# First quad's k and q loaded as f32 on two hardware queues, k in natural key order, batch-0 masks added on TensorE

## The chip, the cores and the metric

One core of one Trainium2 chip. The metric is the device time of one execution in microseconds (us). Nearly all executions of one kernel agree within 1%. Each ratio uses runs on the same chip in the same rounds. The jobs ran on different chips, so medians of two jobs compare only roughly, and the ratios to the kernel before are the better guide.

## The reference

Two stages, one after the other: attention of eight batches with eight heads, 512 local and 32 global positions each, then a two-layer MoE block of 512 to 2048 to 512 on the 4352 rows.

```python
k_all = np.concatenate([k_g, k_l], axis=2); v_all = np.concatenate([v_g, v_l], axis=2)
out_g = sm(scale * q_g @ k_all^T) @ v_all                    # global rows see every key
mask  = np.abs(pos[:, None] - pos[None, :]) <= 32            # local rows: a band ...
s_ll  = np.where(mask, scale * q_l @ k_l^T, -1e9)
out_l = sm(concat([scale * q_l @ k_g^T, s_ll])) @ v_all      # ... and all global keys
h = x @ w_in                                                 # x: out_g and out_l by rows
out = (h * sigmoid(1.702 * h)) @ w_out
```

## The kernel before

Four heads are a *quad*; a batch has two, `a` and `c`. Each engine executes its instructions in the order in which they are written, so an instruction that waits holds up all behind it on its engine (below, a cast that waits 4.3 us holds up a transpose whose input had been ready for 1.9). The attention of batch 0 has no MoE work to lie beside, so TensorE is not full until it is done. Its calls: Tk transposes of k, S scores, X exponential, M mask, K/XK global keys, ekU/U sums and outputs.

```python
    # loads of batch 0: q of quad 0 as f32 by hardware, k by software DMA (gpsimd)
    nc.scalar.dma_start(out=q32, in_=qf[0][:, 0])
    load_g32(0, "qk")                       # small q_g, k_g as f32, on SP's hardware queue
    load_g32(0, "v", eng=nc.scalar)         # small v_g as f32, on ACT's hardware queue
    for j in range(4):
        load_k(0, 0, j)
    ...
        def Tk(self, cs=(0, 1, 2, 3)):      # k: 32x32 transposes on VectorE
            ...
            nc.vector.transpose(self.kT[:, cs], rk[:, cs])          # contiguous write
        ...
        def M(self, rnd, lo=0, hi=LW):      # mask: multiplies the exponentials on VectorE
            e = self.E[rnd][:, :, at + lo : at + hi]
            nc.vector.tensor_mul(e, e, mask[...].to_broadcast(...))
    ...
    # start of batch 0 (S scores, X exponential, K/XK global keys, ekU/U sums and outputs)
    a.S(0)
    a.X(0)
    a.S(1, split=True, warm=4)
    a.X(1)
    c.ext()
    cast_g32(0, "v")                        # v_g -> bf16 tile rvg, on VectorE
    c.Tk()
    a.K(); a.XK(); a.M(0)
    c.Tq(); c.gg(); c.S(0); c.X(0)
    a.M(1)
    ...                                     # eg, c.K
    a.ekU(0); ... a.U(0); a.R()
    a.ekU(1, 3)                             # first TensorE reader of rvg
    c.S(1); c.X(1, halves=True)
    ...                                     # rest of a's and c's outputs, then MoE of batch 0
```

The softmax here doesn't subtract the row's maximum and nothing guards it: scores larger than these inputs give would overflow.

Of the kernel before, what the change touches and what calls it, by code (L numbers as in the profile page):

```python
# [20 lines left out]
def kernel(  # L21
# [43 lines left out]
    kf = k_l.rearrange("b (u j) (c r t) d -> b j r u c (t d)", j=4, c=4, t=4)  # L65
    vf = v_l.rearrange("b h (c r t) d -> b t r h c d", c=4, t=4)
# [6 lines left out]
    def load(b, us=(0, 1), kq=True):  # L73
        if b not in loaded:
            loaded[b] = (ld.tile([128, 2, 4, 4 * D], BF16, name="rk"),
                         ld.tile([128, 2, 16 * D], BF16, name="rq"))
        if kq:
            for j in (0, 2, 1, 3):
                for u in us:
                    load_k(b, u, j)  # L80
            load_q(b, us)

    def load_k(b, u, j):
        nc.gpsimd.dma_start(out=loaded[b][0][32 * j : 32 * j + 32, u], in_=kf[b, j][:, u])  # L84

    def load_q(b, us):
        s = slice(us[0], us[-1] + 1)
        nc.gpsimd.dma_start(out=loaded[b][1][:, s], in_=qf[b][:, s])
# [3 lines left out]
    def load_v(b, us=(0, 1)):  # L92
        s = slice(us[0], us[-1] + 1)
        hs = slice(4 * us[0], 4 * us[-1] + 4)
        for t in (0, 2, 1, 3):
            p = slice(32 * t, 32 * t + 32)
            nc.gpsimd.dma_start(out=vtiles[b % 2][p, s, :, :, :D], in_=vf[b, t][:, hs])  # L97
# [17 lines left out]
    def load_g32(b, names, hold=False, eng=None):  # L115
        for name, s in (("q", qgf), ("k", kgf), ("v", vgf)):
            if name in names:
                t = g32[b, name] = consts.tile([128, 2, D], F32, name="g32%s%d" % (name, b))
                if hold:
                    nc.vector.memset(t[:, :, 0:1], 0.0)  # L120
                if name == "v":
                    load_turned(eng or nc.sync, t, s[:, 2 * b : 2 * b + 2, :])
                else:
                    (eng or nc.sync).dma_start(out=t, in_=s[:, 2 * b : 2 * b + 2, :])

    def cast_g32(b, names):
        for name, t in (("q", rqg), ("k", rkg), ("v", rvg)):
            if name in names:
                if b:
                    nc.scalar.activation(t[:, 2 * b : 2 * b + 2, :D], g32[b, name], AF.Copy)  # L130
                else:
                    nc.vector.tensor_copy(t[:, 2 * b : 2 * b + 2, :D], g32[b, name])

    load(0, kq=False)
    q32 = ld.tile([128, 16 * D], F32, name="q32", bufs=1)
    nc.scalar.dma_start(out=q32, in_=qf[0][:, 0])
    load_g32(0, "qk")
    load_g32(0, "v", eng=nc.scalar)
    for j in range(4):
        load_k(0, 0, j)  # L140


    mk = consts.tile([32, 208], BF16)
    nc.vector.memset(mk, 1.0)
    for sg, base in ((1, 2 * W + 3), (-1, -3)):
        nc.gpsimd.affine_select(
            out=mk, in_=mk, pattern=[[-sg, 208]], compare_op=ALU.is_ge,
            fill=0.0, base=base, channel_multiplier=4 * sg,
        )
# [14 lines left out]
    keep(62, psP.tile([128, 512], F32, name="w", tag="p"), 128)  # L164
# [9 lines left out]
    mb = consts.tile([128, 16, 12], BF16)  # L174
# [3 lines left out]
    def make_mb():  # L178
        for k in range(4):
            nc.vector.tensor_copy(mb[32 * k : 32 * k + 32],  # L180
                                  mk[:, 3 - k : 195 - k].rearrange("p (r t) -> p t r", t=16))

    def make_mask():
        at = 0
        for c, (r0, nr) in enumerate(WIN):
            lo = r0 - 8 * c + 2
            nc.scalar.activation(
                mask[:, c // 2, at : at + 16 * nr].rearrange("p (t r) -> p t r", t=16),
                mb[:, :, lo : lo + nr], AF.Copy)
            at = (at + 16 * nr) % LW  # L190

    ones32 = consts.tile([128, 32], BF16)
    nc.vector.memset(ones32, 1.0)
    nc.vector.memset(rvg[:, :, D:], 1.0)
    bd = consts.tile([128, 4, 32], BF16)
    nc.vector.memset(bd, 0.0)
    for j in range(4):
        r = (j + 1) % 4
        nc.vector.memset(bd[32 * r : 32 * r + 32, j, :], 1.0)
    for i in range(2):  # L200
        v = consts.tile([128, 2, 4, 4, D + 2], BF16, name="v%d" % i)
        nc.vector.memset(v[:, :, :, :, D:], 1.0)
        vtiles.append(v)
# [10 lines left out]
    def load_rest():  # L214
        load_v(0)
        for part in range(2):
            cs = slice(part * (d_ff // 2), (part + 1) * (d_ff // 2))
            for u in range(2):
                nc.gpsimd.dma_start(out=w_in_sb[:, part, 2 * u : 2 * u + 2, :], in_=w_in_r[u][:, :, cs])
        for g4 in range(4):  # L220
            nc.gpsimd.dma_start(
                out=w_out_sb[:, 4 * g4 : 4 * g4 + 4, :].rearrange("p (g e) m -> p g (e m)", e=2),
                in_=w_out_r[:, 2 * g4 : 2 * g4 + 2, :])
            if g4 == 1:
                load(1, (0,))
        load(1, (1,))
        load_v(1, (0,))
        load_v(1, (1,))
        load(2)
# [7 lines left out]
    class Quad:  # L237
        def __init__(self, Q):
# [10 lines left out]
            self.E = [None, None]  # L249
            self.st = {}  # L250
# [3 lines left out]
        def Tk(self, cs=(0, 1, 2, 3)):  # L254
            if cs[0] == 0:
                self.kT = att.tile([128, Sl], F32, name="kT", bufs=3)
                self.k = self.kT.bitcast(BF16).rearrange("p (m e) -> p m e", e=2)
            rk = loaded[self.b][0][:, self.u].bitcast(F32).rearrange("p c w -> p (c w)")
            cs = slice(128 * cs[0], 128 * cs[-1] + 128)
            nc.vector.transpose(self.kT[:, cs], rk[:, cs])  # L260
# [16 lines left out]
        def S(self, rnd, split=False, warm=0):  # L277
            if split:
                ps = [pbank("s") for _ in range(4)]
                keep(warm, ps[0])  # L280
            else:
                pt = self.spt(rnd)
                ps = [pt[:, j, :] for j in range(4)]
            off = 0
            for c in (2 * rnd, 2 * rnd + 1):
                r0, nr = WIN[c]
                t0, n = (0, 4, 1, 4)[c], (20, 19, 19, 20)[c]
                for e in range(2):
                    for j in range(4):
                        p = slice(32 * j, 32 * j + 32)  # L290
                        nc.tensor.matmul(  # L291
                            ps[j][:, off : off + n * nr],
                            lhsT=self.k[p, 128 * c : 128 * c + 128, e],
                            rhs=self.q[p, t0 : t0 + n, r0 : r0 + nr, e],
                            start=(e == 0), stop=(e == 1), skip_group_check=True,
                        )
                off += n * nr
            if split:
                self.gk(ps[2][:, RW : RW + 32], self.qg)
            self.ps = ps if split else pt  # L300
            self.E[rnd] = att.tile([128, 4, RW + 32], BF16, name="e%d" % rnd)
# [12 lines left out]
        def X(self, rnd, halves=False):  # L314
# [6 lines left out]
            for lo, hi in ((0, 228), (228, RW)) if halves else ((0, RW),):  # L321
                nc.scalar.activation(e[:, :, lo:hi], self.ps[:, :, lo:hi], AF.Exp, scale=scale)  # L322
# [3 lines left out]
        def M(self, rnd, lo=0, hi=LW):  # L326
            at = 36 if rnd else 40
            e = self.E[rnd][:, :, at + lo : at + hi]
            nc.vector.tensor_mul(e, e, mask[:, rnd : rnd + 1, lo:hi].to_broadcast([128, 4, hi - lo]))  # L329
# [184 lines left out]
    rk, rq = loaded[0]  # L514
    def cast_q(hf):
        f = slice(512 * hf, 512 * hf + 512)
        nc.scalar.activation(rq[:, 0, f], q32[:, f], AF.Copy)

    make_mb()
    cast_q(0)  # L520
    cast_q(1)
    make_mask()
    cast_g32(0, "q")
    transpose_g(0, 2, "q")
    a.ext((0, 1))
    a.Tq(0, 8)
    a.Tq(8, 16)
    a.Tk((0, 1))
    a.ext((2, 3))
    a.Tk((2, 3))  # L530
    cast_g32(0, "k")
    transpose_g(0, 2, "k")
    load_rest()
    a.S(0)
    a.X(0)
    a.S(1, split=True, warm=4)
    a.X(1)
    c.ext()
    cast_g32(0, "v")
    c.Tk()  # L540
    a.K()
    a.XK()
    a.M(0)
    c.Tq()
    c.gg()
    c.S(0)
    c.X(0)
    a.M(1)
    load_g32(1, "qkv", hold=True)
    a.eg()  # L550
    c.K(0)
    a.ekU(0)
    c.K(1)
    c.XK()
    a.U(0)
    a.R()
    a.ekU(1, 3)
    c.S(1)
    c.X(1, halves=True)
    a.ekU(2, 4)  # L560
    a.U(1)
    a.U(2)
    a.Gm()
    c.M(0)
    a.XL(0)
    c.M(1, 0, 192)
    c.M(1, 192)
    a.XL(1)
# [25 lines left out]
    for fc in range(4, FC):  # L594
        h_step(0, fc)
        if fc == 7:
            cast_g32(1, "qkv")
        if fc == 10:
            transpose_g(2, 4)
# [13 lines left out]
    a.T()  # L613
    a.ext()
# [160 lines left out]
```

## Time and profile before

| | before |
|---|---|
| median of 3 runs | 312.8 us (312.46 to 313.14) |
| span of the profiled run | 310.7 us |
| first exponential starts | 8.61 us |
| MoE of batch 0 starts on TensorE | 20.19 us |
| from that moment to the end | 290.5 us |

After 20.19 us TensorE has next to no hole (its list of waits holds 0.3 us of them), so a change in the start shows in the moment at which MoE starts, and what is left (span less that moment) should stay at 290.5. In some traces the record of MoE's first matmul is missing, so that 15 matmuls stand beside 16 weight loads; the start is then that of the first weight load. Where both are recorded they start together.

### The profile page before, as it was taken

What the parts mean: (1) busy time and instruction counts of PE and PEld (TensorE: products, weight loads), DVE (VectorE), ACT (ScalarE), POOL (GpSimd) and SP (SyncE); (2) the same over time, 40 slices, a digit from 0 to 9 for tenths busy, and PEclk for the clock granted to TensorE, in tenths of its full rate; (3) what the DMA queues carried; (4) which work ended last, traced back from release to release, by engine and by line L of the source; (5) the groups of instructions that cost most, each with busy time, mean ns of one, the idle gap of its engine ahead of it and who ended that gap; (6) DMA issues with size and microseconds to landing.
All of it is one profiled execution on the core that took longest, in us unless ns stands there. A gap on an engine that the chain in (4) does not pass through costs nothing.

```text
span 310.7 us, 7885 instructions
## 1 busy us (share of the span) xinstructions
PE 302.8 (97%) x3257; PEld 148.6 (48%) x3257; DVE 210.4 (68%) x463; ACT 167.3 (54%) x254; POOL 80.0 (26%) x131
## 2 busy tenths in 40 slices
PE   7899999999999999999999999999999999999995
PEld 6444444444554454444454455444454454446653
DVE  7887946869867866776957866776767855574320
ACT  4817465476536744565446735565556652563321
POOL 8822579677146000900045001200000000000000
PEclk9999999999999999999999999999999999999999
DMA  8999999999969212970279113901120012201123
GB/s 154 149 189 207 206 161 193 165 147 129 151 77 168 45 36 61 139 108 12 60 77 169 30 36 71 102 0 31 41 49 23 0 38 55 48 0 29 41 61 76
DMA packets 60099, 27.44 MB, mean 88 GB/s; under 512 B 43296, under 2 KB 51744, under 8 KB 60064
## 3 DMA queue, kind: packets, MB, share of 16 engines
q0 software_dynamic: 51536, 17.11, 50.7%
q1 hardware_dynamic: 7904, 9.12, 11.9%
q10 hardware_dynamic: 624, 0.72, 0.8%
q8 instruction: 25, 0.41, 0.5%
q14 instruction: 10, 0.08, 0.1%
HBM read 35.13 MB, written 8.91 MB: 142 GB/s over the span
## 4 chain that ended last, share of the span: by engine, by line
PE 91%; DVE 3%; ACT 2%; DMA 1%; POOL 1%; issue 0%; ACTq 0%; DVEq 0%; POOLq 0%
PE op L482 37%; PE hp L457 36%; PE s L291 6%; PE ov L389 5%; PE ov L367 3%; DMA rk<-in_k_l_dram 1%; PE s L457 1%; ACT e L322 1%; PE kb L310 1%; DVE e L329 1%; PE op L494 1%; PE s L310 1%; DVE gT L465 1%; PE s L406 1%; POOL rk L84 1%; PE ov L162 1%
## 5 line engine op out<-in xcount | busy, mean ns | idle before, releaser
L482 PE MATMUL op<-w_out_sb,gT 128*128 128x512 bf16 x528 | 121.9, 380 | 0.1
L465 DVE SCALAR_TENSOR_TENSOR gT<-th,hp 128x512 bf16<-128x512 f32 (+1 forms) x140 | 91.1, 655 | 43.0 <-ACT th L464 42.4
L457 PE MATMUL hp<-xL,w_in_sb 128*128 128x512 bf16 x496 | 108.6, 379 | 0.3 <-DVE xL L421 0.3
L464 ACT ACTIVATE th<-hp 128x512 f32<-128x512 f32 (+1 forms) x140 | 79.9, 573 | 43.7 <-PE hp L457 41.2
L457 PEld LDWEIGHTS <-w_in_sb 128*128 128x128 bf16 x576 | 56.1, 98 | 65.1 <-issue 1.2
L482 PEld LDWEIGHTS <-gT 128*128 128x128 bf16 x528 | 49.3, 98 | 56.2 <-issue 3.3
L322 ACT ACTIVATE e<-s 128x1712 bf16<-128x1712 f32 (+2 forms) x32 | 49.6, 1552 | 15.8 <-PE s L406 8.9
L496 ACT ACTIVATE ob<-op 128x512 f32<-128x512 f32 (+2 forms) x35 | 20.5, 585 | 61.6 <-PE op L482 59.1
L97 POOL DMA_DIRECT2D v<-in_v_l_dram x36 | 27.0, 757 | 96.2 <-PE s L406 88.9
L84 POOL DMA_DIRECT2D rk<-in_k_l_dram x64 | 34.9, 557 | 12.3 <-DMA w_in_sb<-in_moe_w_in_dram 4.7
L329 DVE TENSOR_TENSOR e<-e,mask 128x1408 bf16<-128x1408 bf16 (+2 forms) x33 | 28.0, 851 | 6.9 <-ACT e L322 6.7
L412 DVE STREAM_TRANSPOSE sT<-ov 128x512 f32<-128x512 f32 x16 | 11.4, 714 | 31.3 <-PE ov L389 31.3
L291 PE MATMUL s<-q,kT 32*128 32x200 bf16 (+1 forms) x512 | 21.3, 284 | 1.5 <-DVE kT L260 0.9
L421 DVE TENSOR_TENSOR xL<-ov,rs 128x512 bf16<-128x512 f32 x32 | 20.7, 685 | 2.2 <-PE ov L389 0.9
L291 PEld LDWEIGHTS <-kT 32*128 32x128 bf16 x512 | 10.9, 95 | 14.7 <-issue 9.1
L357 ACT ACTIVATE ek<-kb 128x512 bf16<-128x512 f32 x16 | 9.6, 600 | 8.4 <-PE kb L310 8.4
L389 PE MATMUL ov<-e,v 128*32 128x192 bf16 (+1 forms) x512 | 13.1, 240 | 0.0
L416 DVE STREAM_TRANSPOSE rs<-rT 128x512 f32<-128x512 f32 x16 | 11.4, 711 | 0.6
L260 DVE STREAM_TRANSPOSE kT<-rk 128x512 f32<-128x512 f32 (+1 forms) x17 | 11.4, 671 | 0.0
L263 DVE STREAM_TRANSPOSE q<-rq 128x512 f32<-128x512 f32 (+1 forms) x17 | 10.9, 647 | 0.0
L389 PEld LDWEIGHTS <-v 128*32 128x32 bf16 x512 | 9.8, 97 | 2.0 <-issue 2.0
L310 PE MATMUL kb<-q,kgT 32*32 32x512 bf16 x128 | 10.0, 385 | 0.5 <-ACT e L319 0.5
(71 smaller groups left out, 155.5 us busy)
## 6 DMA issues: line engine op xcount, KB each, us to landing
out_dram<-ob SPq DMA_DIRECT2D x132, 64.0 KB, 1.7
rk<-in_k_l_dram POOLq DMA_DIRECT2D x64, 64.0 KB, 4.0
v<-in_v_l_dram POOLq DMA_DIRECT2D x28, 128.0 KB, 4.5
rq<-in_q_l_dram POOLq DMA_DIRECT2D x6, 512.0 KB, 6.7
w_in_sb<-in_moe_w_in_dram POOLq DMA_DIRECT2D x4, 512.0 KB, 11.7
w_out_sb<-in_moe_w_out_dram POOLq DMA_DIRECT2D x4, 512.0 KB, 13.4
rq<-in_q_l_dram POOLq DMA_DIRECT2D x3, 256.0 KB, 7.9
q<-in_q_l_dram ACTq DMA_DIRECT2D x1, 512.0 KB, 3.9
```

Of the source, the lines that this page charges most:

```text
L84: nc.gpsimd.dma_start(out=loaded[b][0][32 * j : 32 * j + 32, u], in_=kf[b, j][:, u])
L97: nc.gpsimd.dma_start(out=vtiles[b % 2][p, s, :, :, :D], in_=vf[b, t][:, hs])
L291: nc.tensor.matmul(ps[j][:, off : off + n * nr], lhsT=self.k[p, 128 * c : 128 * c + 128, e], rhs=self.q[p, t0 : t0 + n, r0 : r0 + nr, e], ...
L322: nc.scalar.activation(e[:, :, lo:hi], self.ps[:, :, lo:hi], AF.Exp, scale=scale)
L329: nc.vector.tensor_mul(e, e, mask[:, rnd : rnd + 1, lo:hi].to_broadcast([128, 4, hi - lo]))
L389: nc.tensor.matmul(ov[32 * j : 32 * j + 32, :].rearrange("p (t r) -> p t r", t=16)[:, :, r0 : r0 + nr], lhsT=lv, rhs=self.E[c // 2][:, j, ...
L421: nc.vector.tensor_mul(self.x[:, 2 * self.u + h, :], self.st[1 + h], self.st["rs"])
L457: nc.tensor.matmul(hp[:, : width(i)], lhsT=w_in_c[:, fc // 8, kc, fc % 8 // 2, :, fc % 2], rhs=(xL[i] if i < B else xG)[:, kc, :], start=( ...
L464: nc.scalar.activation(th[:, :n], hp[:, :n], AF.Tanh, scale=0.851)
L465: nc.vector.scalar_tensor_tensor(gTs[i][:, fc, :n], in0=th[:, :n], scalar=1.0, in1=hp[:, :n], op0=ALU.add, op1=ALU.mult)
L482: nc.tensor.matmul(op, lhsT=gTs[i][:, fc, tci * 128 : tci * 128 + 128], rhs=w_out_sb[:, fc, :], start=(first and fc == 4 * f4), stop=(fc = ...
L496: nc.scalar.activation(ob[:, lo:hi], op[:, lo:hi], AF.Copy, scale=0.5)
```

## The change

Its intent: start earlier. k of the first quad no longer comes by software DMA; k and q come as f32 in halves on both hardware queues. k lies in natural key order, so its transposes write with a step of 16 elements. The masks of batch 0 are added before the exponential, as a bias matmul on TensorE, in place of a multiplication on VectorE after it. The core of the diff:

```diff
-    kf = k_l.rearrange("b (u j) (c r t) d -> b j r u c (t d)", j=4, c=4, t=4)
+    kf = k_l.rearrange("b (u j) (r t) d -> b (j r) u (t d)", j=4, t=16)
 ...
-    nc.scalar.dma_start(out=q32, in_=qf[0][:, 0])
-    load_g32(0, "qk")
-    load_g32(0, "v", eng=nc.scalar)
-    for j in range(4):
-        load_k(0, 0, j)
+    load_g32("q", qgf)
+    for eng, f in ((nc.scalar, halves[0]), (nc.sync, halves[1])):
+        eng.dma_start(out=k32[:, f], in_=kf[0][:, 0, f])
+        eng.dma_start(out=q32[:, f], in_=qf[0][:, 0, f])
+    load_g32("k", kgf)
 ...
-            nc.vector.transpose(self.kT[:, cs], rk[:, cs])
+            nc.vector.transpose(self.kT.rearrange("p (r t) -> p t r", t=16)[:, lo:hi], rk...)
 ...
+        def B(self, rnd, split=False):      # bias: identity x band, opens the accumulation
+                    nc.tensor.matmul(ps[j][...], lhsT=ident, rhs=near(bias, c), start=..., stop=False)
 ...
     a.ext((2, 3))
-    a.Tk((2, 3))
-    cast_g32(0, "k")
+    load_g32("v", vgf, hold=True)           # hold: a memset on VectorE must run first
+    cast_g32("k", rkg)
     transpose_g(0, 2, "k")
     load_rest()
-    a.S(0)
+    a.B(0)
+    a.B(1, split=True)
+    a.S(0, added=True, part=0)
+    a.S(0, added=True, part=1)
     a.X(0)
-    a.S(1, split=True, warm=4)
+    a.S(1, split=True, added=True)
     a.X(1)
+    c.Tk()
     c.ext()
-    cast_g32(0, "v")
-    c.Tk()
+    c.Tq()
+    cast_g32("v", rvg)
+    c.B(0)
     a.K()
     a.XK()
-    a.M(0)
 ...  (quad c's second round likewise; mask copies moved into MoE of batch 0; the second
      batch's small rows by software DMA; v and w_in in other pieces)
```

## The prediction

> **What bounds the kernel now.** I read the page first: the busy table and its 40 slices.
>
> ```profile
> PE 302.8 (97%) x3257; PEld 148.6 (48%) x3257; DVE 210.4 (68%) x463; ACT 167.3 (54%) x254; POOL 80.0 (26%) x131
> PE   7899999999999999999999999999999999999995
> DMA  8999999999969212970279113901120012201123
> ```
>
> TensorE is the bound, and from the second slice on it has no hole; the DMA engines are full in the first 11 slices (85 us). The change cannot touch the MoE matmuls, which are most of the 302.8 us, so it can only bring forward the moment at which TensorE becomes continuously busy with useful work. The page counts the warming matmuls of L162 as busy, so I looked for that moment in the chain in order of time:
>
> ```profile
> 1.35 1.73 POOL rk L84 x3
> 3.08 3.98 DMA rk<-in_k_l_dram
> 7.13 0.38 DVE q L263
> 7.51 0.34 DVE kT L260
> 7.90 0.69 PE s L291 x16
> 8.61 1.61 ACT e L322
> 10.24 0.89 DVE e L329
> ...
> 17.59 0.88 DVE e L329 x2
> 18.51 0.25 PE ov L389 x4
> ...
> 20.26 3.56 PE s L457 x16
> ```
>
> The first scores wait for k (software DMA, landing at 7.06), then two short transposes; the first useful matmul is at 7.90. From there to 20.2, where MoE of batch 0 starts, the chain goes back and forth between the engines; two of its links are mask multiplications (L329). After 20.2 nearly every link is PE: what the change gains must be gained before 20.2. The timeline of the same stretch gives ScalarE and the second quad:
>
> ```profile
> 8.61 1.60 ACT L322 ACTIVATE e<-s 128x1712 bf16<-128x1712 f32 x1 [1.65 <-PE s L291]
> 10.15 1.81 ACT L319 ACTIVATE e<-s 128x428 bf16<-128x428 f32 x4
> 11.83 0.63 ACT L357 ACTIVATE ek<-kb 128x512 bf16<-128x512 f32 x1
> 12.52 1.60 ACT L322 ACTIVATE e<-s 128x1712 bf16<-128x1712 f32 x1
> 15.19 1.66 ACT L322 ACTIVATE e<-s 128x912 bf16<-128x912 f32 x2 [0.49 <-PE s L291]
> 17.51 0.95 DVE L329 TENSOR_TENSOR e<-e,mask 128x768 bf16<-128x768 bf16 x2
> 20.19 3.63 PE L457 MATMUL s<-xL,w_in_sb 128*128 128x512 bf16 x16
> ```
>
> ScalarE is packed from 8.61 to 14.7 (first exponential to the second XK), pauses 0.49, and ends the last exponential at 16.85. Then two mask pieces (ending at 18.46) and 1.73 us of TensorE (half of the sums, then units 1 and 2) lead to 20.19.
>
> Last, whether weights are there when TensorE comes for them. The view of the tile w_in_sb in the first 40 us:
>
> ```profile
> DMA to landing us min/median/max: 8.4/11.7/14.9
> ```
>
> The four transfers were issued from 10.39 to 12.49; the last lands at about 12.49 + 14.9 = 27.4. TensorE needs that one (second half of the columns, kc 2) at 24.03 + 16 x 0.217 + 2 x 0.217 = 27.9. So weights arrive half a microsecond ahead.
>
> **What the Trainium skill says.** ScalarE: Activation LUTs, What ACT_TABLE_LOAD costs: an ACTIVATE with immediate scale and bias takes 186 ns + 0.833 ns an element. For 1712 elements that is 1.61 us; the trace has 1.60. VectorE: DVE Perf Modes, The perf-mode tier table: a copy from f32 in SBUF runs at 2 elements a cycle, tensor_tensor on bf16 at 2 and on f32 at 1. The trace agrees for the mask (1408 elements, 0.873 us mean, 0.62 ns each). DMA: Bandwidth & Descriptors, Issuing engines are not separate DMA queues: transfers from all three queues run on the same 16 engines and interleave, so using two hardware queues saves issue time only. The trace before cannot test it; its hardware queue moved at up to 384 GB/s in the microsecond 3 to 4. The same page, Specifications: below 512 B a transfer does read-modify-write; the page here counts 43296 of 60099 packets under 512 B, and in 6 to 9 us (512 B pieces of k) the engines moved only 117 to 127 GB/s.
>
> **Part by part.**
> *First loads.* Before: q (512 KB, f32) by hardware, k by four software DMAs, 6 to 7.06. After: k and q as f32, four pieces of 256 KB, k first. Bytes: 1.05 MB and 0.13 MB of small q_g and k_g. By the slices, 0.56 MB were moved by 4.0 us, and the rate then was 384 GB/s. k (0.59 MB with q_g) is thus there at about 4.3 to 4.7; the rest, 0.6 MB at 384 GB/s, at 5.6, and as the second quad's software DMAs now start at about 3.0 and share, I take 5.5 for q's first half and 5.9 for its second.
> *ScalarE.* Three casts of 128x512 at 0.6 us (before: two): k at 4.35 and 4.96, q's first half 5.55 to 6.15.
> *VectorE.* Transposes of k's halves (0.42 each) end at 6.0. Cast of q's second half: from the 128x128 casts (182 ns) and 2 elements a cycle I estimate 0.38 us, 6.0 to 6.4. Transposes of q 6.4 to 6.8 and 6.8 to 7.15. Scores' last part ends at 7.5, first exponential starts at **7.6 in place of 8.61: gain 1.0**. k's transposes now write with a step of 16 elements. They are 0.70 us for the contiguous form; the before kernel's strided read (L180, 192 elements in 0.324 us) shows little penalty, so I keep 0.70.
> *ScalarE's run* is unchanged: from the first exponential to the second XK's end took 14.69 - 8.61 = 6.08.
> *Masks of batch 0.* VectorE loses 0.89 + 0.89 + 0.85 + 0.95 = 3.6 us of multiplications and 1.3 us of mask building (L180), ScalarE 1.07 us of mask copies; four mask copies come back in MoE of batch 0, where it idles about 0.27 us a step. Only the last 0.95 us plus two waits, 16.85 to 18.46 = 1.61 us, lies on the path.
> *Bias on TensorE.* 32 matmuls with 128x128 weights, about 0.089 us each by the 62 warming ones (5.49 us), so 0.7 us a round, 2.8 in all. Rounds 1 and 2 fall into the wait for q; warming is shortened by 22 matmuls (1.9 us) and loses its later 11. Round 3 lies beside an exponential. Only the last round is on the path: its PSUM banks come free when the second quad's first exponential is done, 5.72 after the first one's start. Bias 0.7, then scores to exponential 0.72 (14.47 to 15.19 before): start at 7.17, where before it was 6.58. The exponential in one piece takes 1.6, ends at 8.77 against 8.24 before.
> *Sum.* MoE starts 8.77 + 0.05 + 1.73 = 10.55 after the first exponential, before 20.19 - 8.61 = 11.58: gain 1.03. With the 1.0 from the loads, MoE starts at **7.6 + 10.55 = 18.15, which is 2.04 us earlier**.
> *Weights.* k by 4 KB in place of 1 KB at the source, the hardware start, and no four-piece loads ahead: q of the second quad lands near 8.2 against 10.6, so the stream behind it runs about 2.4 us earlier, and w_in's last part lands near 25. It is needed at 25.9. The first 512 columns come first and land near 15, long before 18.15.
> *Later batches.* Same arithmetic; k's DMAs go from 64 to about a dozen, off the path. The only TensorE holes after 35 us sum to about 0.5 us (40 to 70 us), and of these I give the change 0.2 us. VectorE now transposes batch 1's global rows just before its scores, 0.44 us, in about 0.5 us of slack.
> Total: 2.04 + 0.2 = 2.2; 312.8 - 2.2 = **310.6 us**.
>
> **The rivals.**
> (a) *The f32 loads land late.* Twice the hardware bytes, and now shared with the second quad's software DMAs. For it: the small g32 loads, sharing with q32, took 4.3 us to land. If q lands at 6.9, the exponential starts at 8.6, and only the mask's 1.03 is left: 311.6.
> (b) *Weights become the wait.* TensorE comes 2 us earlier, but with 0.5 us to spare before, anything that keeps the DMA stream at its old times gives back 1.5 of the 2.0: 312.2. For it: DMA is full for 85 us. Against: the stream starts with fewer, larger pieces.
> (c) *Bias matmuls eat the gain.* If they run at half that rate, or are held by their banks, the last round costs 1.4, not 0.7, and the result is 311.3. Against: the warming matmuls of the same shape of weights do 0.089.
> (d) *Strided transposes are slow.* If writing with a step doubles k's 0.70, the second quad's scores slip by some 0.3 us and the first by up to 0.4; later batches have VectorE at 68%: 311.3.
> (e) *All goes better:* q lands at 5.2, which gives another 0.5, and the 40 to 70 us holes close: 309.8.
>
> **Range and chances.** Most rivals subtract 0.7 to 1.6 from a gain of 2.2 and one adds 0.8; run noise is 0.35. So 309.3 to 312.0 for 8 in 10. Faster by over 2% needs 6.3 us, half of all there is between 7.9 and 20.2: 0.03. Slower by over 2% would need a hole in steady state: 0.02. Within: 0.95.
>
> **What would show it.** Right: k's casts from about 4.4, first exponential at 7.6 (7.3 to 8.1), ScalarE packed from there, bias of the last round about 0.7 us just after the second quad's first exponential, no VectorE mask before 30 us, first L457-type matmul at 18.2 (17.4 to 18.8), and a steady state without new holes. Wrong: q landing after 6.5; a wait on w_in_sb or w_out_sb between 18 and 42 us; k's transposes at 1 us or more; a hole after 50 us.

## The result, and the profile after

| | before | after |
|---|---|---|
| median of runs of the same rounds | 312.97 us (312.46 to 314.58) | 316.74 us (315.88 to 317.53) |
| ratio after / before | | 1.0111, 95% interval 1.0063 to 1.0159 |
| span of the profiled run | 310.7 us | 315.5 us |
| first exponential starts | 8.61 us | 9.19 us |
| MoE starts | 20.19 us | 24.16 us |
| from there to the end | 290.5 us | 291.3 us |

Slower by 1.1%: within 2%, as the prediction held likely, but 6 us from its 310.6 and outside its range. A ratio here and below is the mean time of one kernel's fast runs over that of the other's fast runs of the same rounds, so not quite the ratio of the medians quoted.

The page of the changed kernel, the rows that answer to those of before (busy time by engine, then tenths in 40 slices of 7.9 us):

```profile
PE 303.6 (96%) x3272; PEld 149.3 (47%) x3272; DVE 210.6 (67%) x447; ACT 167.7 (53%) x251; POOL 55.9 (18%) x90
PE   6779999999999999999999999999999999999994
PEclk9779999999999999999999999999999999999999
DMA  7999999999139511990149312900211012200222
```

The steady state looks as before. The second and third slices differ: TensorE is 0.7 busy there, and its granted clock, 0.9 in every slice before, is 0.7. The chain of waits of the changed kernel, in order of time (start, us, what), over the same stretch:

```profile
1.80 5.73 DMA q<-in_q_l_dram
...
9.25 8.03 DMA g32v<-in_v_g_dram
...
24.23 3.56 PE s L460 x16
```

Two transfers carry it in this stretch: q's second half, which the prediction had, and **g32v**, the 64 KB of v_g, which it did not. Its second part is issued at 9.25 and takes 8.03 us. The timeline shows what stood behind it (start, us, engine, line, tiles; in brackets the idle time before and what ended it):

```profile
9.19 1.60 ACT L325 ACTIVATE e<-s 128x1712 bf16<-128x1712 f32 x1 [2.56 <-PE s L295]
10.75 0.23 DVE L117 CAST rkg<-g32k 128x128 bf16<-128x128 f32 x1 [1.92 <-DMA g32k<-in_k_g_dram]
17.39 0.23 DVE L117 CAST rvg<-g32v 128x128 bf16<-128x128 f32 x1 [4.32 <-DMA g32v<-in_v_g_dram]
17.67 0.40 PE L370 MATMUL ov<-ek,rvg 32*32 32x512 bf16 x4 [1.94 <-DVE rvg L117]
20.30 1.60 ACT L325 ACTIVATE e<-s 128x1712 bf16<-128x1712 f32 x1 [3.74 <-PE s L295]
24.16 3.63 PE L460 MATMUL s<-xL,w_in_sb 128*128 128x512 bf16 x16
```

VectorE stood 4.3 us before a cast of 0.23 us; TensorE then stood 1.9 us before the first matmul that reads rvg; and ScalarE, which the prediction had packed, waited 3.7 us for the scores written behind it. The view of all that TensorE waited for (us in total, times, longest):

```profile
PE ov L370 <- DVE rvg L117: 1.9, 1, 1.9
PE s L314 <- DVE kgT L201: 1.7, 1, 1.7
PE s L295 <- DVE q L257: 1.5, 1, 1.5
PE s L295 <- DVE q L267: 0.4, 1, 0.4
```

The second line is the other small load, g32k. The DMA issues of the first 10 us (size, median us to landing) have both:

```profile
g32k<-in_k_g_dram SPq DMA_DIRECT2D x1, 64.0 KB, 8.5
g32v<-in_v_g_dram SPq DMA_DIRECT2D x1, 48.0 KB, 7.9
```

Before, issued at 0.8 to 1.8 us, they took 4.2 to 4.7, and the cast of v_g waited for nothing:

```profile
9.00 0.22 DVE L132 CAST rvg<-g32v 128x128 bf16<-128x128 f32 x1
```

One more line of the profile of before, which the prediction does not use, had the warning: the same load for batch 1, issued on SP's queue at 13 to 15 us, took 13.1 us to land, where nobody waited for it.

Weights were not the wait: no matmul of MoE waited for w_in_sb; its transfers landed 8.8 to 11.9 us after their issue at 6.8 to 13.3:

```profile
DMA to landing us min/median/max: 8.8/9.8/11.9
```

### The profile page after: what moved, and what is told of

It reads as the page before. It is cut to its first block, busy times and chain, and to the rows that moved or that the text cites. A ratio compares the mean times of both kernels' runs of the same rounds, so it can differ in the third digit from the quotient of the medians.

```text
span 315.5 us, 7823 instructions
## 1 busy us (share of the span) xinstructions
PE 303.6 (96%) x3272; PEld 149.3 (47%) x3272; DVE 210.6 (67%) x447; ACT 167.7 (53%) x251; POOL 55.9 (18%) x90
## 4 chain that ended last, share of the span: by engine, by line
PE 88%; DMA 4%; DVE 3%; ACT 1%; SPq 0%; issue 0%; ACTq 0%; DVEq 0%
PE op L485 36%; PE hp L460 34%; PE s L295 6%; PE ov L392 5%; PE ov L370 3%; DMA g32v<-in_v_g_dram 3%; DMA q<-in_q_l_dram 2%; PE s L460 1%; DVE gT L468 1%; PE kb L314 1%; PE op L497 1%; PE s L314 1%; PE s L409 1%; ACT e L325 1%; DVE q L257 0%; ACT th L467 0%
## 5 line engine op out<-in xcount | busy, mean ns | idle before, releaser
L325 ACT ACTIVATE e<-s 128x1712 bf16<-128x1712 f32 x31 | 49.5, 1597 | 20.3 <-PE s L409 8.9
L89 POOL DMA_DIRECT2D v<-in_v_l_dram x32 | 23.8, 754 | 129.1 <-PE s L409 116.0
L332 DVE TENSOR_TENSOR e<-e,mask 128x1408 bf16<-128x1408 bf16 x28 | 24.4, 871 | 5.5 <-ACT e L325 5.5
L295 PE MATMUL s<-q,kT 32*128 32x228 bf16 (+5 forms) x528 | 21.6, 285 | 1.9 <-DVE q L257 1.5
L253 DVE STREAM_TRANSPOSE kT<-rk 128x512 f32<-128x512 f32 (+1 forms) x17 | 16.9, 992 | 1.0 <-ACT rk L518 0.9
L370 PE MATMUL ov<-ek,rvg 32*32 32x512 bf16 x128 | 10.6, 384 | 1.9 <-DVE rvg L117 1.9
L257 DVE STREAM_TRANSPOSE q<-rq 128x512 f32<-128x512 f32 (+1 forms) x17 | 10.8, 640 | 0.0
L314 PE MATMUL kb<-q,kgT 32*32 32x512 bf16 x128 | 10.8, 413 | 0.0
```

The source lines that it names most:

```text
L89: nc.gpsimd.dma_start(out=vtiles[b % 2][p, s, :, :, :D], in_=vf[b, g][:, hs])
L295: nc.tensor.matmul(ps[j][:, off : off + n], lhsT=self.k[p, 128 * c : 128 * c + 128, e], rhs=self.q[p, lo:hi, r0 : r0 + nr, e], start=(e == ...
L325: nc.scalar.activation(e[:, :, :RW], self.ps[:, :, :RW], AF.Exp, scale=scale)
L332: nc.vector.tensor_mul(e, e, mask[:, rnd : rnd + 1, :].to_broadcast([128, 4, LW]))
L370: nc.tensor.matmul(ov[32 * j : 32 * j + 32, :], lhsT=lv, rhs=self.ek[p], start=True, stop=False, skip_group_check=True)
```

## The experiments

The theory: **one moved load, g32v, costs most of it.** It enters the DMA engines when they are full of software DMA traffic, and VectorE waits for it in order. Rivals: (1) the low clock is the cause, not a companion; (2) the strided transposes; (3) the bias matmuls; (4) the f32 loads of k and q; (5) the small size of g32v's pieces (256 B), rather than the queue it stands in.

For each run: X0 is the start of the first exponential, MoE the start of MoE on TensorE, rest the span of the profiled run less MoE. The column "before" is its median in the same job. A star marks a MoE start taken from the first weight load.

| run | us | before | ratio (95%) | X0 | MoE | rest |
|---|---|---|---|---|---|---|
| gv_early | 312.12 | 312.58 | 0.9977 (0.996 to 0.9993) | 8.54 | 18.88* | 291.7 |
| before_gv_late | 316.02 | 312.91 | 1.0085 (1.0049 to 1.0121) | 8.62 | 23.56* | 291.2 |
| gk_early | 316.55 | 312.58 | 1.0121 (1.0106 to 1.0136) | 10.59 | 23.51* | 291.3 |
| gkv_early | 316.37 | 312.58 | 1.0112 (1.0094 to 1.013) | 11.02 | 22.64* | 291.3 |
| k_flat | 316.42 | 312.58 | 1.0109 (1.0076 to 1.0141) | 9.66 | 24.41* | 290.9 |
| gv_flat | 312.52 | 312.91 | 0.9985 (0.9949 to 1.0022) | 9.63 | 20.12* | 291.0 |
| natural_only | 312.54 | 312.91 | 0.9985 (0.9957 to 1.0014) | 8.58 | 20.16* | 290.8 |
| gv_dve_mask | 313.83 | 312.91 | 1.0016 (0.9983 to 1.005) | 8.99 | 20.98* | 291.3 |
| f32_only | 318.46 | 312.84 | 1.016 (1.0121 to 1.0198) | 12.29 | 26.43* | 290.4 |
| big_packets | 314.99 | 312.84 | 1.0065 (1.0025 to 1.0105) | 10.15 | 22.72* | 291.3 |
| v_behind | 318.13 (1 run) | 312.64 | | 8.64 | 25.28 | 291.1 |
| gv_sw_late | 312.23 | 312.64 | 0.9988 (0.9973 to 1.0003) | 8.77 | 19.39 | 291.2 |
| after_warm | 317.94 | 312.84 | 1.0161 (1.0129 to 1.0193) | 10.07 | 26.10* | 291.2 |
| after_warm2 | 315.52 | 312.64 | 1.0101 (1.0077 to 1.0126) | 8.85 | 22.57 | 291.1 |
| gv_s_later | 311.66 | 312.84 | 0.9968 (0.9937 to 0.9999) | 9.83 | 20.50* | 290.5 |

The last column stays within 290.4 to 291.7 while MoE moves by 7.5 us: what the change did is decided in the start.

### gv_early: the load put back

The changed kernel, with g32v issued on ACT's hardware queue right behind q, without the hold:

```diff
     load_g32("k", kgf)
+    tv = g32["v"] = consts.tile([128, 2, D], F32, name="g32v")
+    load_turned(nc.scalar, tv, vgf[:, 0:2, :])
 ...
-    load_g32("v", vgf, hold=True)
```

> The changed kernel with one thing undone: g32v is issued at about 2 us on the ScalarE queue behind q's first half, without the hold, instead of at 8.9 us on the SyncE queue. Theory (late small hardware loads): the VectorE wait for g32v (4.3 us) and TensorE's 1.9 us wait before unit 1 go, MoE of batch 0 starts near 21.5 instead of 24.2, and the time falls by 2 to 3 us against the changed kernel, to about 314. The wait for g32k until 10.7 stays. Rival (the granted clock of 0.70 to 0.84 between 10 and 25 us is the cause, the waits only its companion): time falls by under 1 us. Rival (the masks' bias matmuls are the cause): no change.

Measured: 312.12 us. In the same job k_flat, which keeps the late load, took 316.42, and the changed kernel itself, in another job, 316.74: **4.3 to 4.6 us come back with one load** (4.2 by the ratios). The f32 loads, the strided transposes and the bias matmuls are all still in gv_early, and it is no slower than the kernel before, so rivals (2), (3) and (4) are not what the change lost. The timeline of gv_early:

```profile
8.54 1.60 ACT L327 ACTIVATE e<-s 128x1712 bf16<-128x1712 f32 x1 [1.57 <-PE s L297]
10.52 0.31 DVE L117 CAST rvg<-g32v 128x128 bf16<-128x128 f32 x1
15.47 1.60 ACT L327 ACTIVATE e<-s 128x1712 bf16<-128x1712 f32 x1 [0.98 <-PE s L297]
18.88 3.14 PEld L462 LDWEIGHTS <-w_in_sb 128*128 128x128 bf16 x16
19.11 3.40 PE L462 MATMUL s<-xL,w_in_sb 128*128 128x512 bf16 x15 [0.16 <-issue]
```

The cast waits for nothing. MoE starts at 18.88 (16 weight loads, 15 matmuls on record), 18.88 - 8.54 = 10.34 us after the first exponential; the prediction worked out 10.55. The other three runs that keep the bias matmuls and the early v_g behind q at a full clock (gv_flat, gv_sw_late, gv_s_later) have 10.49 to 10.67; gkv_early, at a clock of 0.50 in 10 to 15 us, has 11.62. So the masks' part of the prediction was right in size once the load is out of its way; the granted clock is 1.00 in every 5 us of the start, so the low clock came with the waits.

Setting the two starts side by side, each from its own first exponential, divides the 24.16 - 18.88 = 5.28 us: the first exponential 0.65 later (q's second half landed at 7.5, not 6.7); from there to quad c's first exponential 1.41 more (5.19 against 3.78: the wait for k_g, and slower matmuls); from that to the first matmul that reads rvg 2.49 more (3.29 against 0.80: the wait for g32v); and 0.73 more from there to MoE (6.49 against 5.76, matmuls at the low clock). These are differences of starts between two single profiles, so each carries the variation of the landings; q and k_g landed early in this profile of gv_early, which the moved load does not explain.

A second pair is cleaner. k_flat and gv_flat, introduced below, also differ in the place of g32v, and there q's second half (7.8 us in both) and k_g (10.8 and 10.3) landed nearly alike. The casts of v_g, k_flat's first:

```profile
17.33 0.23 DVE L117 CAST rvg<-g32v 128x128 bf16<-128x128 f32 x1 [4.44 <-DMA g32v<-in_v_g_dram]
12.30 0.18 DVE L117 CAST rvg<-g32v 128x128 bf16<-128x128 f32 x1
```

MoE starts 4.29 us apart. Of these, 2.98 lie between quad c's first exponential and the first reader of rvg (3.79 against 0.81), 0.89 behind that, and only 0.42 before. By the ratios the pair differs by 3.9 us.

### before_gv_late: the load moved in the kernel before

The kernel before, with this one move and its cast behind `c.Tq()`:

```diff
-    load_g32(0, "v", eng=nc.scalar)
 ...
+    load_g32(0, "v", hold=True)
     cast_g32(0, "k")
 ...
     c.Tq()
+    cast_g32(0, "v")
```

> The kernel before with only g32v's issue moved as the change moves it: from 1.3 us on the ScalarE queue to about 8.5 us on the SyncE queue, and its cast behind the second quad's q. If a small hardware load that is issued into the software stream lands 7 to 9 us later whatever the kernel, it lands at 16 to 17.5, TensorE waits some 1.5 to 3 us for rvg, and the time is 314.5 to 316, that is most of the change's 3.5 us reproduced by one line. Rival (it was the change's other loads that delayed g32v): lands by 12, time within 0.5 of before.

Measured: 316.02, 3.1 us over before (2.7 by the ratio), with nothing else of the change in it. The first line is of the timeline, the second of TensorE's waits:

```profile
14.09 0.23 DVE L132 CAST rvg<-g32v 128x128 bf16<-128x128 f32 x1 [2.33 <-DMA g32v<-in_v_g_dram]
PE ov L388 <- DVE g32v L120: 1.9, 1, 1.9
```

The second line names a memset because that stands last in front of TensorE's release. What TensorE waited for here was not rvg but the second mask multiplication, which stood behind the cast in VectorE's order: it ran at 14.23 us, where the kernel before had it at 12.00. So the cast hurt by its place on an in-order engine, before any reader of rvg was due. The load landed 5.1 us after its issue, earlier than the 8 of the changed kernel, and the loss was smaller. With gv_early this shows the theory from both sides: taking the late load out of the changed kernel removes the loss, and putting it alone into the kernel before brings most of it. Both edits move the load between the queues of ACT and SP as well as in time; no run has it early on SP's queue or late on ACT's, and none has the late load with its cast further back.

### gk_early and gkv_early: the other small load

g32k in front of k and q on SP's queue; gkv_early has g32v early too.

```diff
     load_g32("q", qgf)
+    load_g32("k", kgf)
     for eng, f in ...
-    load_g32("k", kgf)
```

> The changed kernel with g32k issued ahead of k and q on the SyncE queue (at 1.3 instead of 2.3 us); g32v stays late. Theory: the cast of k_g no longer waits until 10.7, the second quad's transposes and scores come 1 to 1.5 us earlier, but VectorE and TensorE then still wait for g32v at about 17, so MoE of batch 0 starts within 0.7 us of the changed kernel's 24.2 and the time hardly moves (315.5 to 317). If the g32k wait is the one that ends last: 1.5 us faster. k's and q's second halves should land about 0.4 us later.

> Both: g32k ahead of k and q, g32v behind q's first half on the ScalarE queue. Theory: both waits go; first exponential at about 9.3 to 9.6, ScalarE packed from there, MoE of batch 0 starts at 10.6 after it, that is near 20; the time is about that of the kernel before (312 to 313.5), 3.5 to 4 us under the changed one. The granted clock between 10 and 25 us should come back to near 1. Rival (clock or bias matmuls): stays over 315.

gk_early hit its time (316.55) but not its reason: k's and q's second halves landed 2.1 and 1.4 us later than in the changed kernel, not 0.4, and quad c's first exponential came later, not earlier. gkv_early, which should have been the best, missed with 316.37. The first line is of its DMA issues, the second of TensorE's waits:

```profile
q<-in_q_l_dram SPq DMA_DIRECT2D x1, 256.0 KB, 6.9
PE s L297 <- DVE q L259: 2.7, 1, 2.7
```

k_g did come early, but behind its 64 KB of 256 B pieces k's half on the same queue landed at 7.2 and q's at 9.2, where gv_early had 5.8 and 6.7. X0 went from 8.54 to 11.02, and with the long wait the clock was 0.50 in 10 to 15 us. The order on the hardware queue is all that gk_early changes: a small load ahead of the large ones cost them 1.4 to 2.5 us in these two runs. One on the other queue behind q cost nothing that stands out of the spread of landings. So g32k's place at the end of SP's queue, though it causes the 1.7 us wait of the changed kernel, is the better of the two once g32v is early (gkv_early against gv_early); with g32v late, the two places end alike (316.55 against 316.74).

### k_flat, gv_flat and natural_only: natural order and the strided transposes

k_flat is the changed kernel, gv_flat is gv_early, with the transposes writing contiguously. Their keys are then in a wrong order; the comparison with the reference still passed, so its tolerance doesn't see this error. natural_only is the kernel before with the natural key order and what belongs to it: k of a quad in one load, v grouped to match, strided transposes, masks cut from the new band.

```diff
-            nc.vector.transpose(self.kT.rearrange("p (r t) -> p t r", t=16)[:, lo:hi], rk...)
+            nc.vector.transpose(self.kT[:, 32 * lo : 32 * hi], rk...)
```

> The changed kernel with k's 32x32 transposes writing contiguously again instead of with a step of 16 elements; the key order and so the result are wrong on purpose. Theory: each 128x512 transpose takes 0.70 instead of 1.04 us; the 0.43 us hole of TensorE at 70 us goes, and the time falls by 0.3 to 0.6 us. Rival (strided writes are the main cause): falls by 2 us or more.

> gv_early with k's transposes writing contiguously; key order wrong on purpose. If the strided writes cost what gv_early lost after MoE's start (it starts 1.1 us ahead of the kernel before and ends 0.4 ahead), the time falls by 0.4 to 0.8 us below gv_early, to about 311.5, and the scores of batch 1's second-next quad come within 9.0 us of that stage's start instead of 9.7. Rival (no path passes through them): within 0.2 us of gv_early.

> The kernel before with only the key order changed: k in one 4 KB-a-row software load per quad, strided transposes, masks from the band by multiplication; q f32 on hardware and the small loads as before. Theory: k lands a little earlier or the same (7.0), second quad's about 1 us earlier, transposes cost 0.34 us more each; the time within 0.7 of before (312.0 to 313.5). Rival (natural order alone brings the software stream forward enough to be worth it): 311.5 or less.

The groups of VectorE by form, the changed kernel first and then k_flat (last columns: busy us, mean ns, idle before):

```profile
L253 DVE STREAM_TRANSPOSE kT<-rk 128x512 f32<-128x512 f32 x15 | 15.6, 1043 | 0.0
L253 DVE STREAM_TRANSPOSE kT<-rk 128x512 f32<-128x512 f32 x15 | 10.5, 703 | 0.0
```

The step of 16 elements costs 0.34 us a transpose, 48%. It reaches TensorE in one place, at batch 1's first scores, as VectorE comes late with the last copies into q. natural_only and the changed kernel wait 0.4 us there; in gv_early it is longer:

```profile
65.42 0.66 PE L297 MATMUL s<-q,kT 32*128 32x200 bf16 x16 [0.87 <-DVE q L269]
```

In k_flat and gv_flat, which like the changed kernel transpose batch 1's global rows late, this wait is gone; so there the strided writes make it, not the moved transposes of global rows. They are not the only thing that can: before_gv_late, with contiguous transposes, waits 0.40 us at the same place. k_flat still lost 3.4 us by its ratio, so rival (2) is not the cause of the loss. In the times it is at the edge of what can be seen: gv_flat started MoE 1.24 us later than gv_early and ended only 0.4 later (medians), its rest is 291.0 against 291.7. Natural order alone (natural_only) gains nothing and loses nothing that was resolved.

### gv_s_later: moving the reader instead

gv_early, with batch 1's next scores one step of 16 later in MoE, so that VectorE has time (5 rounds):

```diff
-        if fc == 9:
+        if fc == 10:
             a.S(0)
 ...
-        if fc == 12:
+        if fc == 13:
             a.M(0)
```

> gv_early with the scores of the next batch one step later in batch 1's MoE (behind the 10th in place of the 9th column block, mask behind the 13th). TensorE's 0.87 us wait for VectorE there goes; if nothing else takes its place, the time is 0.4 to 0.9 us under gv_early, 311.3 to 311.8, so 0.3% under the kernel before. Rival (VectorE's backlog turns up at the mask or in the next scores): no gain.

Measured: 311.66 us, ratio 0.9968 to before: the fastest version here, if barely, and correct as far as the comparison sees. No wait for q is left after the start, its rest is 290.5, and its profiled start was even 1.6 us later than gv_early's. A start like gv_early's with this rest would make 18.88 + 290.5 = 309.4 of span, some 1.3 us under before; that is an estimate, and no run had both.

### gv_dve_mask: bias against multiplication

gv_early with batch-0 masks by multiplication on VectorE again (mask copies on ScalarE at the start, no bias matmuls; the emission order otherwise nearly that of gv_early):

```diff
-    a.B(0)
-    a.B(1, split=True)
-    a.S(0, added=True, part=0)
+    a.S(0, part=0)
 ...
+    a.M(0)
-    c.S(0, added=True)
+    c.S(0)
```

> gv_early with batch 0's masks back on VectorE as multiplications (copies built in ScalarE's waits for q), no bias matmuls. My prediction gave the bias 1.0 us of gain: so about 1.0 us slower than gv_early, 313.1, with MoE starting at 20.1 instead of 19.1. Rival (the bias matmuls are worth nothing, since the last round's 0.7 us cancels the mask): within 0.3 us of gv_early.

Measured: 313.83, 1.7 us over gv_early's median (1.2 by the ratios); MoE starts 11.99 us after the first exponential, against 10.34. That is the gain that the bias was to bring (the prediction had 1.03), and more. But it isn't a clean size, as the windows view of gv_dve_mask shows (length, busy us of PE, PEld, DVE, ACT and POOL with their instructions, then the granted clock, the DMA share and GB/s):

```profile
10.00:15.00 5.00, 3.89 (x72) 1.51 (x72) 4.12 (x12) 4.26 (x7) 3.18 (x5) 0.50 1.92 176
```

Without the bias matmuls TensorE stood idle ahead of the scores and ran the next stretch at half clock. k_g also landed later there, at 10.0 us against 8.3. So the bias matmuls may do two things: take the mask off VectorE, and keep the clock up while q is on its way; the second fits but was not tested apart. Either way rival (3) falls: bias made the start shorter.

### f32_only: the hardware loads without natural order

The kernel before, with k of the first quad as f32 on the two hardware queues but in the old layout, so in 1 KB pieces; the small k_g and v_g now stand behind k and q:

```diff
-    nc.scalar.dma_start(out=q32, in_=qf[0][:, 0])
+    for eng, js, h in ((nc.scalar, (0, 1), 0), (nc.sync, (2, 3), 1)):
+        for j in js:
+            eng.dma_start(out=k32[32 * j : 32 * j + 32], in_=kf[0, j][:, 0])
+        eng.dma_start(out=q32[:, ...], in_=qf[0][:, 0, ...])
 ...
-    for j in range(4):
-        load_k(0, 0, j)
```

> The kernel before with only the first quad's k moved to the hardware queues as f32 (in the old layout, four pieces of 128 KB, two on each queue, ahead of q; g32k and g32v behind). Old masks, old key order. Theory from gv_early: k lands at 4 to 6, q's second half at 6.5 to 8, so the first exponential does not start earlier than 8.3, the last one ends as before, and the time is within 0.7 of before; k_g and v_g, small and last, land at 8 to 10. Rival (the hardware k is the gain): 311.5 or less.

Missed: 318.46. The last of k's four loads landed only at 7.2 us (5.5 in the changed kernel; the other three by 4.4), and ScalarE's table load of 1.28 us, which otherwise lies at 1.8 us beside the transfers, came after k's landing at 7.33. So X0 is 12.29. The run says that these loads gained nothing in the old layout; how much of the loss is the late load, how much its 1 KB pieces and how much the table load is not separated. So it says little of rival (4), which gv_early answers.

### big_packets and v_behind: what holds the load up

Two edits of the changed kernel. big_packets loads v_g late as 32 rows of 2 KB, not 256 B pieces (a wrong result, relative error 0.25). v_behind issues the software loads of v, in small pieces, behind w_in's first blocks, so that g32v meets a stream of larger pieces (1 KB).

```diff
+            nc.sync.dma_start(out=v32, in_=v_g[0].rearrange("h (a s) d -> (h a) (s d)", a=4))
-            load_turned(nc.sync, t, src[:, 0:2, :])
```

```diff
-        for u in range(2):
-            for p in (slice(0, 64), slice(64, 128)):
-                nc.gpsimd.dma_start(out=vtiles[0][p, u, :, :, :D], in_=vp[u, p])
         ... (first 512 columns of w_in)
+            (the same four loads here)
```

> The changed kernel with its late 64 KB load at the same place and on the same queue, but as 32 rows of 2 KB (2 for each DMA engine) in place of 256 pieces of 256 B (16 for each engine), into another tile; the values are wrong on purpose. If each piece waits its turn behind a packet of the software stream, few pieces land in 3 us or less (by 12), TensorE's 1.9 us wait before unit 1 goes, and the time is 2 to 4 us under the changed kernel (313 to 314.5). Rival (the hardware queue as such is held up behind the software stream, whatever the pieces): lands at 16 to 17, time as the changed kernel.

> The changed kernel with batch 0's v (128 B pieces) in the software stream behind w_in's first four blocks (1 KB pieces) in place of ahead of them; g32v is issued at 8.9 us as in the changed kernel. If it is v's stream of small packets that keeps the hardware queue from its turn (nothing of g32v moves between 9 and 13 us in the changed kernel), g32v now lands by 13, 4 us sooner; the time does not tell, as v itself comes at about 18 and becomes the wait. Rival (any software stream does it): g32v lands at 16 or later again.

In big_packets the load, issued at 9.84, landed 6.6 us later. In v_behind it landed 6.8 to 6.9 us after its issue at 8.3 and 8.7, and nothing of it moved before 11 to 12 us though the stream's pieces were then larger. (v_behind is slower in all, as v itself then became a wait of 1.8 us; one look.) In these profiles neither the load's own pieces nor the stream's make the difference. But big_packets' time, 314.99, met neither expectation: it is 1.4 us under the changed kernel by the ratios, and two of its four runs took 313.66 and 314.27, while the profile is of one that took 315.72. So rival (5) is not the main cause in what was seen, and a part of it stays open. The moved pieces, counted by queue and microsecond in the changed kernel: from 10 to 13 us the hardware queues moved 2, 0 and 0 pieces (k_g landed in the first of these microseconds) and the software queue 1068, 1114 and 795. The line of 11 to 12 us (pieces, MB, time of the pieces as a share of the 16 engines' time; no hardware queue is listed):

```profile
q0 software_dynamic: 1114, 0.14, 372.3%
```

An early issue does not mean a quick landing: g32k, issued at 2.3 us just ahead of the stream, took 4.8 to 9.0 us in the runs, and the early g32v 4.6 to 7.4. It means that the load is there before VectorE comes for it.

### gv_sw_late: is q late because of the software stream?

gv_early with three dummy fills on GpSimd ahead of the second quad's loads, which delay the software stream by some 2.5 us.

```diff
+    pad = consts.tile([128, 1024], BF16)
+    for _ in range(3):
+        nc.gpsimd.memset(pad, 0.0)
     load(0, (1,))
```

> gv_early with the second quad's software loads (and all behind them) issued some 2.5 us later, by three fills of an unused tile on GpSimd. If the software stream slows k and q (they land at 5.8 to 8.3 in the gv kernels where I had predicted 4.7 and 5.9), q's second half lands at 6.3 or earlier and the first exponential starts at 8.0 or earlier, k_g by 8. Rival (1.05 MB with 0.19 MB of 256 B pieces takes so long by itself): q's second half at 6.7 or later as in gv_early. The time: within 1 us of gv_early either way, as second quad, v and weights come later.

q's second half landed at 1.80 + 4.8 = 6.6, k's at 5.8, k_g at 7.1. So 6.6 is what the hardware transfers take by themselves, and the prediction's 5.9 was out of reach. (The software queue moved nothing before 6.6 us in this profile.) The 7.5 to 8 of other runs, and k_g's 10.7 in the changed kernel, had the software stream beside them; but so had gv_early, with 6.7, so the stream is not shown to be what makes q late.

### after_warm and after_warm2: how much is the clock

The changed kernel with dummy matmuls and repeated bias matmuls in its waits. after_warm had too many: they outlasted the waits. after_warm2:

```diff
+                keep(20, ps[2][:, 460:512], 52)
 ...
-    a.B(0)
+    for _ in range(3):
+        a.B(0)
 ...
-    a.ekU(1)
+    a.ekU(1, 4)
```

> The changed kernel with its waits left in, but dummy matmuls in TensorE's three waits (bias of round 0 repeated four times, 44 narrow ones before the k_g scores, 9 before unit 1), so that the granted clock stays up. If the drop of the clock to 0.70-0.84 (10 to 25 us) is a part of the loss: granted clock 0.95 or more in that stretch and 0.7 to 1.3 us faster than the changed kernel, near 315.5. If the clock only accompanies waits that end by DMA: within 0.3 us of it.

> after_warm with fewer dummy matmuls, sized to fit into the waits (bias three times, 20 narrow ones, 4 before unit 1). If the lower clock is a part of the loss, MoE starts at 22.8 to 23.5 (24.2 in the changed kernel) with a granted clock of 0.95 or more between 10 and 20 us, and the time is 0.5 to 1.2 us under the changed kernel's. If not: within 0.3 us of it.

after_warm gave 317.94 with the clock still at 0.69 in 15 to 20 us: inconclusive. after_warm2 had 1.00 from 5 to 25 us, where the changed kernel has 0.70 to 0.84 from 10 to 25, and took 315.52: 1.2 us better than the changed kernel's median, 0.3 by the ratios (1.0101 against 1.0111), and 3 us still lost. Its profile also had k_g landing at 7.2 by itself, so neither the clock nor the late k_g is what those 3 us are; VectorE's wait for g32v, 4.8 us, was still there. The clock is a small part, 0.3 to 1.2 us and not resolved, and rival (1) is not the cause.

## Why the prediction was wrong

**The step that failed: the list of what the change moves.** The prediction priced the large loads, the casts, the masks and the weights, and took VectorE from the first exponential on as lighter than before. It left out that the small g32v goes from about 1.3 us to 8.9, and that g32k goes behind q. Its sentence "ScalarE's run is unchanged" rests on VectorE and TensorE being in time, and the rvg cast stands between them. That term, taken as zero, was about 4 us: 3.9 (k_flat against gv_flat) to 4.6 (the changed kernel against gv_early). Nor was g32v among the rivals or in the list of what would make it wrong. The diff and the order of instructions had it: a load moved behind a `hold`, to be read some microseconds later in the middle of a stream whose transfers took 8 to 15 us to land.

**The size of what is then left.** MoE was to start at 18.15 and started at 24.16: 1.59 of the 6.01 is the first exponential (9.19 for 7.6), 4.42 the rest (14.97 for 10.55). gv_early takes the second to 10.34.

**First loads: mechanism right, size off.** k's halves landed at 3.9 and 5.5 (4.3 to 4.7 predicted), q's first at 5.6 (5.5), but q's second at 7.5 (5.9), and 6.6 even without the software stream. The step assumed 384 GB/s until the last byte; in the changed kernel the engines moved 393 in the microsecond 3 to 4, but 229, 222 and 162 in the next three. (The prediction also read the 117 to 127 GB/s of 6 to 9 us as those of 512 B pieces; from 8 to 9 us 50 of the 91 pieces were of 2 KB or more, and the rate was 117 all the same.) "q landing after 6.5" was on the list of what would make it wrong, and did: it is rival (a), which in full gave up the first 1.0 us of gain. In gv_early the first exponential is at 8.54 against 8.61, so of the gain from the loads nothing is left.

**ScalarE's and TensorE's masks: right.** 10.34 for 10.55 in gv_early, and not by luck of the sum: the last exponential ended 8.53 after the first one's start (8.77 predicted), and MoE followed 1.81 later (1.78). The bias of the last round took 0.77 us in gv_early (0.7 predicted), 0.99 at the low clock of the changed kernel.

**Strided transposes: wrong, and rival (d) right in its mechanism.** 1.04 us in place of the 0.70 kept. The reason given was a strided read of bf16 with little penalty; a strided write of f32 is another thing. The Trainium skill, SBUF — State Buffer, Door 1: The DMA port swizzle, has a note that I had not drawn on: SBUF lines are 16 bytes, each access that crosses into a new line pays, so f32 may step by up to 4 elements for free. A step of 16 is beyond that, and the 1043 against 704 ns agree. The cost in time is small: 0.4 us of wait in the changed kernel, 0.9 in gv_early, at the place where the prediction counted on 0.5 us of slack.

**Weights in time: right.** No wait on w_in_sb or w_out_sb; rival (b) didn't come. (The second quad's q landed at 11.0 us, not near 8.2, but nothing waited for it.) The bias matmuls didn't eat the gain; rival (c) fell.

**Where the expected gain went.** Of 2.2 us, gv_early has 20.19 - 18.88 = 1.31 at MoE's start. Its rest, where the prediction had 0.2 to gain, is 1.2 longer than before's, 0.87 of it the wait at 65.42. Its spans are thus equal to before's to 0.1, and its time 0.5 better. gv_s_later takes that wait out and is 0.3% faster than before.

**Open.** The landing of q's second half and of k_g differs between kernels that are alike up to that point (6.6 to 8.1 and 7.1 to 11), and moves the start by about 1 us. Why the hardware queue stands still beside the software stream is not shown, only that it did in the three profiles counted, at each size of piece tried.

## What to carry to other kernels

In a diff, list every load whose place of issue moves, however small, and ask at what microsecond it enters, what the DMA engines are full of then, and which in-order engine stands in front of its first reader: 64 KB cost more here than all of the large loads could gain. Price a moved load with landing times from the same stretch of the trace, where another load on that queue may show them, not from the quiet first microseconds. What served here was to put the small load ahead of the software stream, on a hardware queue behind the large loads that are needed first.

## What the Trainium skill lacked or had wrong

- DMA: Bandwidth & Descriptors, Queues, rings and completion order: each engine is said to take turns between the queues that have work, packet by packet. The runs don't look like a fair turn: of a 64 KB hardware load issued at 8.9 us nothing moved from 11 to 13 us while the software queue moved 1909 pieces, and late loads of this kind took 5.1 to 8.0 us to land, with 256 B or 2 KB pieces. In the kernel before, issued at 0.8 to 1.8 us, they took 4.2 to 4.7. A sentence on how late a small hardware load can be beside software DMA is lacking.
- VectorE: DVE Perf Modes, The three transpose paths: there is one time for a transpose on VectorE, for bf16, and none for a transpose that writes with a step. The trace has 0.70 us for 512 f32 elements written contiguously and 1.04 with a step of 16 elements.
